# One of seven half products of the second layer as three one-pass products, in blocks 2 to 4

## The chip, the cores and the metric

The kernel runs on one core of a Trainium2 chip. The metric is the device time of one launch in microseconds (us); lower is better. Half a dozen queues work side by side on that core: TensorE (PE, with its weight loads shown as PEld), VectorE (DVE), ScalarE (ACT), GpSimd (POOL) and SyncE (SP), which issues the DMAs.

## The reference

A state-space layer (Mamba-2 SSD, chunks of 32 tokens) is followed by a two-layer perceptron with a hard-swish. The inputs of the second part are float64 and are decoded by the kernel to float32.

```python
# x (4, 8, 768, 32), a (4, 8, 768), B and C (4, 8, 768, 16)
for c in range(nc):                                   # chunks
    cum = np.cumsum(log_a[:, :, sl], axis=-1)
    L = np.exp(cum[:, :, :, None] - cum[:, :, None, :]) * causal
    M = np.einsum('bhin,bhjn->bhij', Cc, Bc) * L
    y[:, :, sl] = M @ xc + (Cc @ state) * np.exp(cum)[..., None]
    state = decay_full * state + sum_j(Bc * xc * decay_from_j)
x = y.transpose(0, 2, 1, 3).reshape(3072, 256)        # tokens x (heads * head_dim)
h = x @ w_in                                          # (3072, 2048)
g = h * np.clip(h + 3.0, 0.0, 6.0) / 6.0
out = g @ w_out                                       # (3072, 256)
```

## The kernel before

The 768 positions are cut into six blocks, k = 0 to 5, of 128 positions; a block holds the 512 tokens of the four batches. For a block, the state-space layer gives yT, the first layer gives g for f = 0 to 15 (128 of the 2048 hidden units each; the tile gT is 128 x 16 x 512), and the second layer gives the output. While the perceptron of block k runs, the state-space layer of block c = k + 1 is worked in between, and the decays of block ahead = k + 2 are prepared. The order of all of this is written out by hand: each engine's queue is what the Python loops emit, in that order, and every engine takes its queue strictly in order.

**The first layer in parts.** From block 1 on, the first layer isn't done with four-pass float32 matmuls but with three one-pass matmuls (type F32R) per product: weights and y are split into a high part of 12 bits, a low part, and a third part `less` which holds a combination of both. `squares(k, f)` does high x high and low x low into one PSUM bank, `enlarge(k, f)` multiplies the bank by 2^12 + 1 in place (on ScalarE; for f % 4 == 3 on VectorE), and `cross(k, f)` adds less x less. `factor(k, f)` then makes g: a Relu ramp on ScalarE (`ramp`, L754) and a multiplication on VectorE (`times_ramp`, L759). The loop over f emits `squares(f)`, `cross(f - 2)`, `enlarge(f)`, `factor(f - 2)`. Six banks take turns: f0 to f3, y0, y1.

**The second layer in blocks 1 to 4.** `wide_units(k)` is a Strassen-like scheme with seven half products in place of eight. The hidden units are paired (f = 2j + e, j = 0 to 7), and g is cut into quarters a11, a12, a21, a22 by e and by the half r of the tokens. `g_sums` makes s1 = a21 + a22, a21 = a11 - a21 (in place), s2 = s1 - a11 and s4 = a12 - s2 on GpSimd, two j at a time (L818; a sum of 128 x 512). `weight_sums` makes the sums of w_out once (t, L798). A half product is eight float32 matmuls of 128x256 (`product`, L914). They go to the banks oa, ob (tag o) and oc (tag f2), and the function is a generator: it yields after each of 14 units (i = 0 to 13), and the loop behind it emits other work between them:

- after unit 0 the last cross products, factors and GpSimd's sums;
- after unit 2 (3 for c = 2) `scores(c)`, which fills the banks f0 to f3 (L530), and `multiply(c)`, four VectorE multiplications that read them (L579), bank f2 first;
- after units 3 to 6 `decay_ends`: eight exponentials on ScalarE (L385) and `ends` on GpSimd (L396), for block ahead;
- `results(c)`: `sums`, `mix` (the state-space products on TensorE, L548, L625, L503), `split_y` (y_hi on ScalarE L704, y_lo and y_less on VectorE L705, L707), `take` and `renew` (the state), `from_start(ahead)` and the loads of `rows(ahead + 1)` on SP. It stands after unit 7 for c = 2 and 3, after unit 5 for c = 4 and after unit 6 for c = 5;
- after unit 9 `turn_all(ahead)` (four to five VectorE operations), after unit 12 `lead` and `lead_on`, the first products of the next block.

Between the units, ScalarE and VectorE add up the products: `third` and L967 after unit 9 (which reads both halves of ob), `u2` and L974 after unit 11, L982 after unit 13; `turned_back` transposes into `back`, and `store` issues 16 DMAs of 16 KB on SP, after units 11 and 13. In `conceal`, GpSimd masks the decays of block ahead (L158), which a DMA brought, at f = 3 and 7 (8 and 12 in block 1).

The last block has an order of its own: its second layer is done in one-pass parts as well (`last_out`, L880), 128x256 each.

Of the kernel before, what the change touches and what calls it, by code (L numbers as in the profile page):

```python
# [8 lines left out]
FP32 = mybir.dt.float32  # L9
# [3 lines left out]
F32R = mybir.dt.float32r  # L13
AF = mybir.ActivationFunctionType
ALU = mybir.AluOpType
# [6 lines left out]
def kernel(  # L22
# [24 lines left out]
    nc = tc.nc  # L47
    P = 128
# [3 lines left out]
    NC = S // P  # L52
# [750 lines left out]
    def g_quarter(k, e, r):  # L803
        return gTs[k].rearrange("p (j e) (r i) -> p e r j i", e=2, r=2)[:, e, r]

    def g_sums(k, j0, ops=range(4)):

        if k not in gsums:
            gsums[k] = {n: loads.tile([P, NJ, 2 * P], FP32, name=f"s{n}", tag="raw", bufs=NRAW)
                        for n in (1, 2, 4)}  # L810
        js = slice(j0, j0 + 2)
        a11, a12, a21, a22 = (g_quarter(k, e, r)[:, js] for r in range(2) for e in range(2))
        s1, s2, s4 = (gsums[k][n][:, js] for n in (1, 2, 4))
        sums_ = ((s1, a21, a22, ALU.add), (a21, a11, a21, ALU.subtract),
                 (s2, s1, a11, ALU.subtract), (s4, a12, s2, ALU.subtract))
        for n in ops:
            o, p_, q_, op = sums_[n]
            nc.gpsimd.tensor_tensor(out=o, in0=p_, in1=q_, op=op)  # L818

    out_parts, g_parts, ends_ = {}, {}, {}  # L820

    def split_out(i):
# [82 lines left out]
    def wide_units(k):  # L905


        halves = [[g_quarter(k, e, r) for r in range(2)] for e in range(2)]
        g2, g4, g1 = (gsums[k][n] for n in (2, 4, 1))

        def product(bank, slot, lhs, rhs, js, clear=False):

            for j in js:
                nc.tensor.matmul(  # L914
                    out=bank[:, slot], lhsT=lhs[:, j], rhs=rhs[:, j],
                    start=(clear and j == 0), stop=True, skip_group_check=True)

        near, far = range(NJ // 2), range(NJ // 2, NJ)
        res = ffn.tile([P, 2, 2, 2 * P], FP32, name="wide")
        back = ffn.tile([P, 2, TB], FP32, name="back")  # L920

        def turned_back(m, r=None):

            if r is None:
                o, i = back[:, m], res[:, m].rearrange("p r i -> p (r i)")
            else:
                o, i = back[:, m, r * 2 * P:(r + 1) * 2 * P], res[:, m, r]
            nc.vector.transpose(out=o, in_=i)

        def store(m):  # L930
            for b in range(NB):
                r0 = b * S + k * P
                for q in range(4):
                    c0 = m * P + 32 * q
                    nc.sync.dma_start(
                        out=out[r0:r0 + P, c0:c0 + 32].rearrange("(c i) m -> i c m", i=32),
                        in_=back[32 * q:32 * q + 32, m, b * P:(b + 1) * P].rearrange(
                            "i (c m) -> i c m", m=32))

        oa, ob = (ps_o.tile([P, 2, 2 * P], FP32, name=n, tag="o") for n in ("wa", "wb"))  # L940
        product(oa, 0, w4[:, 0, 0], halves[0][0], near, clear=True)
        yield
        product(oa, 0, w4[:, 0, 0], halves[0][0], far[:-1])
        yield
        product(ob, 0, wsums[4], halves[1][1], near, clear=True)
        yield
        product(ob, 0, wsums[4], halves[1][1], far)
        yield
        oc = ps.tile([P, 2, 2 * P], FP32, name="wc", tag="f2")
        product(oc, 0, w4[:, 1, 0], halves[1][0], near, clear=True)  # L950
        yield
        product(oc, 0, w4[:, 1, 0], halves[1][0], far)
        product(oa, 0, w4[:, 0, 0], halves[0][0], far[-1:])
        nc.scalar.copy(out=res[:, 0, 0], in_=oc[:, 0])
        nc.vector.tensor_tensor(out=res[:, 0, 0], in0=oa[:, 0], in1=res[:, 0, 0], op=ALU.add)
        yield
        product(ob, 1, wsums[1], g1, near)
        yield
        product(ob, 1, wsums[1], g1, far)
        turned_back(0, 0)  # L960
        yield
        product(oc, 1, wsums[3], halves[0][1], near)
        yield
        product(oc, 1, wsums[3], halves[0][1], far)
        third, u2 = (ffn.tile([P, 1, 2 * P], FP32, name=n) for n in ("third", "u2"))
        nc.scalar.copy(out=third, in_=oc[:, 1:2])
        nc.vector.tensor_tensor(  # L967
            out=res[:, :, 1], in0=ob, in1=third.to_broadcast([P, 2, 2 * P]), op=ALU.add)
        yield
        product(oa, 0, wsums[2], g2, near)  # L970
        yield
        product(oa, 0, wsums[2], g2, far)
        nc.vector.tensor_copy(out=u2, in_=oa[:, 0:1])
        nc.vector.tensor_tensor(  # L974
            out=res[:, :, 1], in0=res[:, :, 1], in1=u2.to_broadcast([P, 2, 2 * P]), op=ALU.add)
        turned_back(0, 1)
        store(0)
        yield
        product(ob, 1, w4[:, 1, 1], g4, near)
        yield  # L980
        product(ob, 1, w4[:, 1, 1], g4, far)
        nc.vector.tensor_tensor(out=res[:, 1, 0], in0=ob[:, 1], in1=u2[:, 0], op=ALU.add)  # L982
        turned_back(1)
        store(1)
        yield
# [2 lines left out]
        load_decay(c)  # L988
        load_eto(c)

    def results(c):
        if c >= TURN:
            sums(c)
        mix(c)
        if c == 1:
            keep(c)
        split_y(c)
        if TURN <= c < NC - 1:
            take(c)
        if TURN < c < NC - 1:  # L1000
            renew(c)
# [67 lines left out]
    load_x(1)  # L1069


    weave, g_done = {}, {}
    for i in range(2, NP + 2):
        for j in range(5):
            weave.setdefault(4 * i - 8 + j, []).append(i)
# [1 line left out]
    for k in range(NC):  # L1077
        gTs[k] = ffn.tile([P, NF, TB], FP32, name="gT")
        c, ahead = k + 1, k + 2
        if k == 0:  # L1080
# [14 lines left out]
            for i in range(NP):  # L1095
                for b in range(NB):
                    first_out(b, i, c)
                    for n in w_more.get((i, b), ()):
                        next(ins[n])
                    if (i, b) == (2, 0):  # L1100
                        conceal(ahead, 0)
                        conceal(ahead, 1)
                    if (i, b) == (0, 0):
                        weights(NP + 3, 1)
                        weights(NP + 2, 1)
                        weights(NP + 3, 3)
                    elif (i, b) == (1, 3):
                        turn(c, 1)
                        wake(c)
                        turn(c, 0)  # L1110
                        load_bc(ahead)
                    elif (i, b) == (2, 3):
                        decay(ahead, 0)
                        scores(c)
                        multiply(c)
                        decay(ahead, 1)
                        renew(c)
                        next(ins[2])
                        next(ins[2])
                    elif (i, b) == (3, 1):  # L1120
                        results(c)
                        decay(ahead, 2)
                    elif (i, b) == (3, 2):
                        decay(ahead, 3)
                        from_start(ahead)
                    elif (i, b) == (3, 3):
                        for q in range(NB):
                            ends(ahead, q)
# [25 lines left out]
        for f in range(2, NF):  # L1154
# [11 lines left out]
                conceal(ahead, int(f in (7, 12)))  # L1166
            if c == NC - 1 and f in (6, 8, 9):
                next(outs_[0])
            if f == NF - 1 and k not in gsums:
                g_sums(k, 0, ())  # L1170
            if k > 1 and f in (6, 10, 14):
                g_sums(k, len(g_done.setdefault(k, [])) * 2)
                g_done[k].append(f)
            if k == 1:
                if f in (4, 5, 7):
                    next(ins[3])
# [5 lines left out]
        for i, _ in enumerate(wide_units(k)):  # L1182
            if i == 0:
                cross(k, NF - 1)
                factor(k, NF - 2)
                factor(k, NF - 1)
                for n in range(4):
                    for j in range(len(g_done.get(k, [])) * 2, NJ, 2):
                        g_sums(k, j, (n,))
                if k == 1:  # L1190
                    next(more)
            if c < NC:
                if i == (3 if c == TURN else 2):
                    scores(c)
                    multiply(c)
                if ahead < NC and 3 <= i < 7:
                    decay_ends(ahead, i - 3)
                if i == {TURN: 7, TURN + 1: 7, TURN + 2: 5}.get(c, 6):
                    results(c)
                    if ahead < NC:  # L1200
                        from_start(ahead)
                    if ahead + 1 < NC:
                        rows(ahead + 1)
                if c == NC - 1:
                    for _ in range({5: 2, 8: 1, 9: 2, 10: 1, 11: 1}.get(i, 0)):
                        next(outs_[i // 8])
                if i == 9 and c == TURN:
                    renew(c)
# [36 lines left out]
```

## Time and profile before

| | |
|---|---|
| median of 3 runs | 340.27 us (340.24 to 340.45) |
| the profiled execution, its own time | 339.78 us |
| its span, first to last instruction | 337.6 us |
| TensorE busy, of the span | 330.6 us (98%) |
| VectorE, ScalarE, GpSimd busy | 234.5, 199.4, 123.9 us |
| granted TensorE clock | 1.00 |
| first layer of block 2 (137.6 to 157.6 us) | VectorE 12.3, ScalarE 14.3, GpSimd 12.4 us busy |
| second layer of block 2 (157.6 to 189.0 us) | VectorE 16.5, ScalarE 13.3, GpSimd 14.5 us busy |

The span is counted in microseconds from the first instruction; all positions in the text are on that scale. A block from 2 to 4 takes 51.1 to 51.2 us, so a place in block 2 is found 51.1 us later in block 3 and about 102.3 us later in block 4. A busy time is the union of an engine's instructions; a four-pass float32 matmul leaves two records, a one-pass matmul one.

### The profile page before, as it was taken

Reading aid. Unit: us, or ns where it says so; the run is one execution under the profiler, and the core shown is the slowest. Engines: PE = TensorE matmul, PEld = TensorE weight load, DVE = VectorE, ACT = ScalarE, POOL = GpSimd, SP = SyncE. Lnnn points to the kernel's source line nnn. Section 1 sums busy time; section 2 is a strip of 40 time slices with the busy share of each in tenths; the row PEclk is TensorE's granted clock in tenths of the full one; section 3 lists DMA queues with packets and bytes.
Section 4 is the critical chain, followed back from the end, with each engine's and each line's share of the span. In section 5 each row is a group of like instructions: output and inputs, shape, how many; then the busy total and the mean of one; then the engine's idle time right before and its main releaser. Section 6 shows DMA issues by size and latency. Waiting matters only on the chain.

```text
span 337.6 us, 8192 instructions
## 1 busy us (share of the span) xinstructions
PE 330.6 (98%) x3337; PEld 265.4 (79%) x3337; DVE 234.5 (69%) x380; ACT 199.4 (59%) x418; POOL 123.9 (37%) x123
## 2 busy tenths in 40 slices
PE   6999999999999999999999999999999999999996
PEld 2554448888888888888888888888888888899995
DVE  6699999998399739755339556355477355599974
ACT  4769878757986670576461576570486030577661
POOL 3300000290184799089813079911079800000000
PEclk9999999999999999999999999999999999999999
DMA  8999968042590215258107267101160001110001
GB/s 174 165 316 201 208 219 184 2 54 76 139 142 1 57 37 139 33 72 78 33 13 156 33 83 69 28 4 17 27 81 2 2 2 18 26 21 2 1 2 62
DMA packets 89605, 25.15 MB, mean 75 GB/s; under 512 B 82208, under 2 KB 85952, under 8 KB 89056
## 3 DMA queue, kind: packets, MB, share of 16 engines
q1 hardware_dynamic: 85184, 23.33, 37.5%
q10 hardware_dynamic: 4384, 1.31, 1.8%
q8 instruction: 26, 0.43, 0.5%
q14 instruction: 11, 0.09, 0.1%
HBM read 21.33 MB, written 3.29 MB: 73 GB/s over the span
## 4 chain that ended last, share of the span: by engine, by line
PE 94%; DMA 3%; DVE 1%; SPq 1%; issue 0%; DVEq 0%
PE h L715 33%; PE wb L914 13%; PE wc L914 8%; PE o L772 8%; PE h L647 8%; PE wa L914 8%; PE o_end L880 6%; PE y L625 3%; PE y L503 2%; PE cb L530 2%; DMA raw<-in_moe_w_in_dram 2%; DMA pairs<-in_C_dram 1%; PE y L548 1%; SPq L101 1%; PE o_end L898 1%; PE sp L548 0%
## 5 line engine op out<-in xcount | busy, mean ns | idle before, releaser
L759 DVE SCALAR_TENSOR_TENSOR gT<-gT,h 128x512 f32<-128x512 f32 x96 | 64.8, 684 | 33.8 <-ACT gT L754 32.2
L754 ACT ACTIVATE gT<-h,half 128x512 f32<-128x512 f32 x96 | 65.2, 685 | 25.6 <-PE h L715 23.6
L735 ACT ACTIVATE h<-h 128x512 f32<-128x512 f32 x66 | 38.2, 585 | 39.0 <-PE h L715 38.8
L715 PE MATMUL h<-y_hi,w_part 128*128 128x512 f32 x160 | 51.5, 407 | 0.0
L715 PE MATMUL h<-y_less,w_part 128*128 128x512 f32 x160 | 50.1, 399 | 0.0
L715 PE MATMUL h<-y_lo,w_part 128*128 128x512 f32 x160 | 49.5, 395 | 0.0
L818 POOL TENSOR_TENSOR s<-gT 128x512 f32<-128x512 f32 x16 | 23.8, 1490 | 46.7 <-DVE gT L759 46.7
L715 PEld LDWEIGHTS h<-y_lo,w_part 128*128 128x128 f32 x160 | 30.0, 188 | 7.3
L715 PEld LDWEIGHTS h<-y_hi,w_part 128*128 128x128 f32 x160 | 30.0, 188 | 6.8 <-DVE gT L759 0.2
L715 PEld LDWEIGHTS h<-y_less,w_part 128*128 128x128 f32 x160 | 29.2, 188 | 6.0 <-ACT h L735 0.2
L385 ACT ACTIVATE L<-L,cum_n 128x64 f32<-128x64 f32 x128 | 31.6, 336 | 0.0
L772 PE MATMUL o<-w_out,gT 128*128 128x256 f32 x128 | 28.8, 381 | 0.0
L647 PE MATMUL h<-yT,w_in 128*128 128x512 f32 x64 | 27.7, 594 | 0.0
L772 PEld LDWEIGHTS o<-w_out,gT 128*128 128x128 f32 x128 | 24.1, 190 | 3.8 <-issue 0.5
L647 PEld LDWEIGHTS h<-yT,w_in 128*128 128x128 f32 x64 | 12.1, 190 | 14.9 <-issue 13.2
L158 POOL TENSOR_SCALAR_AFFINE_SELECT L<-L 64x1024 f32<-64x1024 f32 (+1 forms) x16 | 20.4, 1281 | 8.5 <-DMA L<-cum_d 8.0
L579 DVE TENSOR_TENSOR L<-L,cb 128x512 f32<-128x512 f32 x24 | 15.0, 681 | 11.7 <-PE cb L530 11.7
L403 POOL TENSOR_TENSOR tmp<-state,eto 128x256 f32<-128x256 f32 x5 | 3.2, 643 | 52.8 <-ACT eto L389 48.9
L818 POOL TENSOR_TENSOR s<-gT,s 128x512 f32<-128x512 f32 x16 | 21.7, 1364 | 0.9
L396 POOL TENSOR_TENSOR bs<-B,L 128x128 f32<-128x128 f32 x24 | 11.2, 486 | 29.5 <-ACT L L385 20.9
L880 PE MATMUL o_end<-v_pair,g_pair 128*128 128x256 f32 x120 | 21.1, 281 | 0.0
L818 POOL TENSOR_TENSOR gT<-gT 128x512 f32<-128x512 f32 x16 | 20.4, 1279 | 0.9
(140 smaller groups left out, 593.0 us busy)
## 6 DMA issues: line engine op xcount, KB each, us to landing
raw<-in_moe_w_out_dram SPq DMA_DIRECT2D x4, 1024.0 KB
L<-cum_d SPq DMA_DIRECT2D x8, 512.0 KB
xt<-in_x_dram SPq DMA_DIRECT2D x6, 512.0 KB
raw<-in_moe_w_in_dram SPq DMA_DIRECT2D x3, 1024.0 KB
out_dram<-back SPq DMA_DIRECT2D x128, 16.0 KB
pairs<-in_C_dram SPq DMA_DIRECT2D x40, 32.0 KB
eto<-cum_e SPq DMA_DIRECT2D x20, 64.0 KB
B<-in_B_dram SPq DMA_DIRECT2D x5, 256.0 KB
```

Source lines behind the costliest of these rows:

```text
L158: nc.gpsimd.affine_select(out=t[rows], in_=t[rows], pattern=pattern, compare_op=ALU.is_ge, fill=-1e5, base=base, channel_multiplier=-1)
L385: nc.scalar.activation(Ls[c][:, b, h], Ls[c][:, b, h], AF.Exp, bias=cum_n[:, c, g:g + 1])
L579: nc.vector.tensor_tensor(out=Ls[c][:, :, hs], in0=Ls[c][:, :, hs], in1=cbs[c][q], op=ALU.mult)
L647: nc.tensor.matmul(out=h, lhsT=w_in[f // FP][:, j, f % FP * P:(f % FP + 1) * P], rhs=yTs[k][:, j].rearrange("p b i -> p (b i)"), start=(j ...
L715: nc.tensor.matmul(out=hs_[k, f], lhsT=w[j][:, f % FP * P:(f % FP + 1) * P], rhs=y[:, j], start=(start and j == 0), stop=True, skip_group_ ...
L735: nc.scalar.activation(h, h, AF.Copy, scale=1.0 / EPS + 1.0)
L754: nc.scalar.activation(gTs[k][:, f], h, AF.Relu, bias=half, scale=1.0 / 6.0)
L759: nc.vector.scalar_tensor_tensor(out=g, in0=g, scalar=1.0, in1=h, op0=ALU.min, op1=ALU.mult)
L772: nc.tensor.matmul(out=o[:, b % 2], lhsT=gTs[0][:, f, b * P:(b + 1) * P], rhs=w_out[:, f], start=(f == 0 and b % 2 == 0), stop=True, skip_ ...
L818: nc.gpsimd.tensor_tensor(out=o, in0=p_, in1=q_, op=op)
L880: nc.tensor.matmul(out=ends_["cross" if n == 2 else "squares"][b], lhsT=g_parts[t][n][:, b * P:(b + 1) * P], rhs=w, start=(t == 0 and b < ...
L914: nc.tensor.matmul(out=bank[:, slot], lhsT=lhs[:, j], rhs=rhs[:, j], start=(clear and j == 0), stop=True, skip_group_check=True)
```

## The change

In blocks 2 to 4 the half product t4 x a22 (unit 2 and 3 of `wide_units`) is no longer done by eight four-pass matmuls. t4 is split once into three parts (`split_sum`, in block 2), a22 in each block (`split_quarter`), and `exact` does 24 one-pass matmuls: high x high and low x low as unit 6, an enlarging of the bank's half by ScalarE, and less x less as unit 8. Product t1 x s1 takes the places of units 2 and 3. The sum s4 is written over a22, once the parts are made, so the first three of GpSimd's four sums stay where they were and the fourth moves behind unit 3. `results` is cut in two: `own_products` (sums and mix) stays, for c = 5 one unit earlier, and the rest moves behind unit 8. The parts live in tiles that are free at that time (wide, back, y_hi's, y_lo's and y_less's, cT's), so the result tiles wide and back are made only after unit 8, and the first transpose into back moves behind the rest of results.

```diff
     def g_sums(k, j0, ops=range(4)):
-        s1, s2, s4 = (gsums[k][n][:, js] for n in (1, 2, 4))
+        s1, s2, s4 = gsums[1][:, js], gsums[2][:, js], a22 if k > 1 else gsums[4][:, js]
...
+    def split_sum():
+        pair = loads.tile([P, 2, NJ, P], F32R, name="t_pair", tag="raw", bufs=NRAW)
+        hi, lo, t = pair[:, 0], pair[:, 1], wsums[4]
+        cuts = [slice(i * NJ // 2, (i + 1) * NJ // 2) for i in range(2)]
+        for sl in cuts:
+            nc.scalar.activation(hi[:, sl], t[:, sl], AF.Copy, scale=(1.0 - EPS / 2) * EPS)
+            yield
+            nc.vector.scalar_tensor_tensor(
+                out=lo[:, sl], in0=hi[:, sl].bitcast(FP32), scalar=-1.0 / EPS, in1=t[:, sl],
+                op0=ALU.mult, op1=ALU.add)
+            yield
+        less = const.tile([P, NJ, P], F32R, name="t_less", tag=f"w{NP - 1}")
+        for sl in cuts:
+            nc.gpsimd.tensor_tensor(
+                out=less[:, sl], in0=lo[:, sl].bitcast(FP32), in1=hi[:, sl].bitcast(FP32),
+                op=ALU.subtract)
...
+            yield
+
+    def split_quarter(k):
...
+        halves = [g_quarter(k, 1, 1)[:, j * NJ // 2:(j + 1) * NJ // 2] for j in range(2)]
+        hi, lo, less = quarter_parts[k] = [], [], []
+        homes = ((ffn, "wide"), (ffn, "back")), ((const, "w0"), (att, "y_lo"))
+        for where, g in zip(homes, halves):
+            h, l = (home(*w) for w in where)
...
+            for j in range(NJ // 2):
+                nc.scalar.activation(h[:, j], g[:, j], AF.Copy, scale=1.0 - EPS / 2)
+                nc.vector.tensor_tensor(
+                    out=l[:, j], in0=g[:, j], in1=h[:, j].bitcast(FP32), op=ALU.subtract)
+                yield
+        tag = {NC - 2: (ffn, "wide")}.get(k, (att, "cT"))
+        for l, h, where in zip(lo, hi, ((att, "y_less"), tag)):
+            less.append(home(*where))
+            nc.vector.scalar_tensor_tensor(
+                out=less[-1], in0=l.bitcast(FP32), scalar=-1.0 / EPS, in1=h.bitcast(FP32),
+                op0=ALU.mult, op1=ALU.add)
+            yield
...
+        def exact(bank, slot, *pairs):
+            for n in pairs:
+                for j in range(NJ):
+                    nc.tensor.matmul(
+                        out=bank[:, slot], lhsT=sum_parts[0][n][:, j],
+                        rhs=quarter_parts[k][n][j // (NJ // 2)][:, j % (NJ // 2)],
+                        start=False, stop=True, skip_group_check=True)
...
-        product(ob, 0, wsums[4], halves[1][1], near, clear=True)
-        yield
-        product(ob, 0, wsums[4], halves[1][1], far)
+        first_w, first_g = (wsums[1], g1) if parts_ else (wsums[4], halves[1][1])
+        product(ob, int(parts_), first_w, first_g, near, clear=True)
+        yield
+        product(ob, int(parts_), first_w, first_g, far)
...
+        if parts_:
+            exact(ob, 0, 0, 1)
+            nc.scalar.activation(ob[:, 0], ob[:, 0], AF.Copy, scale=1.0 / EPS + 1.0)
+            yield
+        else:
...
         product(oc, 1, wsums[3], halves[0][1], near)
         yield
+        if parts_:
+            exact(ob, 0, 2)
+            yield
+            res = ffn.tile([P, 2, 2, 2 * P], FP32, name="wide")
+            back = ffn.tile([P, 2, TB], FP32, name="back")
+            nc.vector.transpose(out=back[:, 0, :2 * P], in_=u1)
         product(oc, 1, wsums[3], halves[0][1], far)
...
     in the loop over f:
             if k > 1 and f in (6, 10, 14):
-                g_sums(k, len(g_done.setdefault(k, [])) * 2)
-                g_done[k].append(f)
+                g_sums(k, (f - 6) // 2, range(3))
+            if k == 2 and f in (2,3,4,5,6,8):
+                next(t_parts)
+            if k > 1 and f == 2:
+                quarters = split_quarter(k)
+            if k > 1 and f in ((12,13,14,15) if k == 2 else (12,13,14,15)):
+                next(quarters)
...
     between the units (i == 0 is after unit 0):
+                else:
+                    g_sums(k, NJ - 2, (0,))
+                    for _ in range(NJ // 2):
+                        next(quarters)
+            if k > 1 and i == 3:
+                for j, ops in ((4, (3,)), (0, (3,)), (2, (3,)), (6, (1, 2, 3))):
+                    g_sums(k, j, ops)
+            if k > 1 and i in (3, 6 if c == NC - 1 else 6):
+                next(quarters)
...
-                if i == {TURN: 7, TURN + 1: 7, TURN + 2: 5}.get(c, 6):
+                u = {TURN: 7, TURN + 1: 7, TURN + 2: 5}.get(c, 5)
+                if i == u:
+                    own_products(c)
+                if i == (max(u, 8) if c > TURN else u):
                     results(c)
...
                 if c == NC - 1:
-                    for _ in range({5: 2, 8: 1, 9: 2, 10: 1, 11: 1}.get(i, 0)):
+                    for _ in range({6: 1, 7: 1, 8: 1, 9: 2, 10: 1, 11: 1}.get(i, 0)):
                         next(outs_[i // 8])
```

More of the change, by code (lines that the diff above doesn't have):

```diff
@@ L806, in g_sums @@
     def g_sums(k, j0, ops=range(4)):
-        if k not in gsums:
-            gsums[k] = {n: loads.tile([P, NJ, 2 * P], FP32, name=f"s{n}", tag="raw", bufs=NRAW)
-                        for n in (1, 2, 4)}
+        if not gsums:
+            gsums.update({n: loads.tile([P, NJ, 2 * P], FP32, name=f"s{n}", tag="raw", bufs=NRAW)
+                          for n in (4, 1, 2)})
         js = slice(j0, j0 + 2)
         a11, a12, a21, a22 = (g_quarter(k, e, r)[:, js] for r in range(2) for e in range(2))
-        s1, s2, s4 = (gsums[k][n][:, js] for n in (1, 2, 4))
+        s1, s2, s4 = gsums[1][:, js], gsums[2][:, js], a22 if k > 1 else gsums[4][:, js]
         sums_ = ((s1, a21, a22, ALU.add), (a21, a11, a21, ALU.subtract),
@@ L818, in g_sums, with home @@
             nc.gpsimd.tensor_tensor(out=o, in0=p_, in1=q_, op=op)
+    def split_sum():
[14 more added lines that the diff above has]
+                op=ALU.subtract)
+            if sl is cuts[1]:
+                sum_parts.append((hi, lo, less))
+            yield
+    def split_quarter(k):
+        def home(pool, tag):
+            return pool.tile([P, NJ // 2, 2 * P], F32R, name="q_part", tag=tag, bufs=1)
+        halves = [g_quarter(k, 1, 1)[:, j * NJ // 2:(j + 1) * NJ // 2] for j in range(2)]
[3 more added lines that the diff above has]
+            h, l = (home(*w) for w in where)
+            hi.append(h)
+            lo.append(l)
+            for j in range(NJ // 2):
[10 more added lines that the diff above has]
+            yield
+    sum_parts, quarter_parts = [], {}
     out_parts, g_parts, ends_ = {}, {}, {}
@@ L908, in wide_units @@
         halves = [[g_quarter(k, e, r) for r in range(2)] for e in range(2)]
-        g2, g4, g1 = (gsums[k][n] for n in (2, 4, 1))
+        parts_ = k > 1
+        g2, g1 = gsums[2], gsums[1]
+        g4 = halves[1][1] if parts_ else gsums[4]
         def product(bank, slot, lhs, rhs, js, clear=False):
@@ L916, in product @@
                     start=(clear and j == 0), stop=True, skip_group_check=True)
+        def exact(bank, slot, *pairs):
[5 more added lines that the diff above has]
+                        start=False, stop=True, skip_group_check=True)
         near, far = range(NJ // 2), range(NJ // 2, NJ)
-        res = ffn.tile([P, 2, 2, 2 * P], FP32, name="wide")
-        back = ffn.tile([P, 2, TB], FP32, name="back")
+        if not parts_:
+            res = ffn.tile([P, 2, 2, 2 * P], FP32, name="wide")
+            back = ffn.tile([P, 2, TB], FP32, name="back")
         def turned_back(m, r=None):
@@ L953, in wide_units @@
         product(oa, 0, w4[:, 0, 0], halves[0][0], far[-1:])
-        nc.scalar.copy(out=res[:, 0, 0], in_=oc[:, 0])
-        nc.vector.tensor_tensor(out=res[:, 0, 0], in0=oa[:, 0], in1=res[:, 0, 0], op=ALU.add)
+        u1 = ffn.tile([P, 1, 2 * P], FP32, name="u2")[:, 0] if parts_ else res[:, 0, 0]
+        nc.scalar.copy(out=u1, in_=oc[:, 0])
+        nc.vector.tensor_tensor(out=u1, in0=oa[:, 0], in1=u1, op=ALU.add)
         yield
-        product(ob, 1, wsums[1], g1, near)
-        yield
-        product(ob, 1, wsums[1], g1, far)
-        turned_back(0, 0)
-        yield
+        if parts_:
[3 more added lines that the diff above has]
+        else:
+            product(ob, 1, wsums[1], g1, near)
+            yield
+            product(ob, 1, wsums[1], g1, far)
+            turned_back(0, 0)
+            yield
         product(oc, 1, wsums[3], halves[0][1], near)
         yield
+        if parts_:
+            exact(ob, 0, 2)
+            yield
+            res = ffn.tile([P, 2, 2, 2 * P], FP32, name="wide")
+            back = ffn.tile([P, 2, TB], FP32, name="back")
+            nc.vector.transpose(out=back[:, 0, :2 * P], in_=u1)
         product(oc, 1, wsums[3], halves[0][1], far)
@@ L989, in rows, with own_products @@
         load_eto(c)
-    def results(c):
+    def own_products(c):
         if c >= TURN:
@@ L994, in results @@
         mix(c)
+    def results(c):
         if c == 1:
@@ L1069 @@
     load_x(1)
-    weave, g_done = {}, {}
+    weave, t_parts = {}, split_sum()
     for i in range(2, NP + 2):
@@ L1168 @@
                 next(outs_[0])
-            if f == NF - 1 and k not in gsums:
+            if f == NF - 1 and k == 1:
                 g_sums(k, 0, ())
             if k > 1 and f in (6, 10, 14):
-                g_sums(k, len(g_done.setdefault(k, [])) * 2)
-                g_done[k].append(f)
+                g_sums(k, (f - 6) // 2, range(3))
[5 more added lines that the diff above has]
+                next(quarters)
             if k == 1:
@@ L1186 @@
                 factor(k, NF - 1)
-                for n in range(4):
-                    for j in range(len(g_done.get(k, [])) * 2, NJ, 2):
-                        g_sums(k, j, (n,))
                 if k == 1:
+                    for n in range(4):
+                        for j in range(0, NJ, 2):
+                            g_sums(k, j, (n,))
                     next(more)
+                else:
[7 more added lines that the diff above has]
+                next(quarters)
             if c < NC:
@@ L1197 @@
                     decay_ends(ahead, i - 3)
-                if i == {TURN: 7, TURN + 1: 7, TURN + 2: 5}.get(c, 6):
+                u = {TURN: 7, TURN + 1: 7, TURN + 2: 5}.get(c, 5)
+                if i == u:
+                    own_products(c)
+                if i == (max(u, 8) if c > TURN else u):
                     results(c)
```

## The prediction

> **What bounds the kernel now.** I read the page's busy table first, then the chain that ended last, then the chain in order of time, and last the timelines of VectorE and GpSimd around the places that the change touches.
>
> ```profile
> PE 330.6 (98%) x3337; PEld 265.4 (79%) x3337; DVE 234.5 (69%) x380; ACT 199.4 (59%) x418; POOL 123.9 (37%) x123
> ...
> PEclk9999999999999999999999999999999999999999
> ...
> PE 94%; DMA 3%; DVE 1%; SPq 1%; issue 0%; DVEq 0%
> ```
>
> TensorE makes up 94% of the chain, at the full granted clock. From 22.6 us on nothing else of any length stands in the chain until the last result. So every TensorE microsecond removed is a microsecond won, and every late operand is one lost. The other engines cost nothing until TensorE waits for them. Their order and deadlines must be followed, not their shares.
>
> The chain in order of time gives the prices (start, length, records):
>
> ```profile
> 161.05 1.73 PE wb L914 x8
> ...
> 166.32 3.45 PE wc L914 x16
> ...
> 170.20 3.45 PE wb L914 x16
> ...
> 296.42 1.43 PE o_end L880 x12
> 297.85 1.39 PE h L715 x6
> 299.24 1.44 PE o_end L880 x12
> ```
>
> A half product of eight four-pass matmuls leaves 16 records and takes 3.45 us. Twelve one-pass matmuls of the last block, 128x256 as well, take 1.43 us: 0.119 us each, with the change-over from L715 included.
>
> **Step 1, TensorE.** Per block 24 one-pass matmuls take 24 x 0.119 = 2.86 us in place of 3.45: 0.59 us less, 1.78 us in blocks 2 to 4 together. Nothing else enters its queue, and the number of units stays 14. The nearest rows bound the pitch: half the 0.2325 us of the 512-wide L715 gives 0.116 (1.97 us won in all); 0.122, the slowest pair of rows above, gives 1.6.
>
> By the Trainium skill, TensorE: Matmul & The Clock Gate, section Back-to-back issue gap, an isolated warm matmul comes every N/2.4 + 2.5 ns, an estimate of 109 ns here and 2.5 us won; the L880 rows of this trace, at 119 ns, disagree, and they decide.
>
> **Step 2, ScalarE and VectorE during the last four f of a block.** Each adds a ScalarE copy of 128x256 (419 ns in the SBUF row of L704, some 0.3 us queued) and a VectorE subtraction of 128x256 (0.42 us, 0.34 queued, L705). ScalarE idles 0.21 to 0.24 us in three of four f and 0.67 in the fourth, so its lag stays near 0.3 us. An enlarge has about 2.2 us until its cross product, and a bank some 2.5 us until it is reused. ScalarE costs nothing. The constant part of t (two copies, two subtractions of 512 columns) is hidden at the start of block 2 likewise, where VectorE idles 0.7 us per f.
>
> VectorE is not that simple, because GpSimd sums g at the same time. Rows of block 1 show how they meet:
>
> ```profile
> 105.36 1.21 DVE L798 TENSOR_TENSOR t<-w_out,t 128x1024 f32<-128x1024 f32 x1
> ...
> 105.51 2.19 POOL L818 TENSOR_TENSOR s<-gT 128x512 f32<-128x512 f32 x1 [2.44 <-DVE gT L759]
> ...
> 126.32 2.53 DVE L707 SCALAR_TENSOR_TENSOR y_less<-y_lo,y_hi 128x512 fp32r<-128x512 f32 x2
> ...
> 177.44 1.28 DVE L707 SCALAR_TENSOR_TENSOR y_less<-y_lo,y_hi 128x512 fp32r<-128x512 f32 x2
> ```
>
> The GpSimd sum that came 0.15 us after a VectorE operation with two SBUF inputs ended 1.13 us after that one ended: it stood still in between. The two y_less take 1.28 us alone, 2.53 beside sums. Operations that read PSUM beside SBUF (L759, L579) show none of this. So a new subtraction waits until the running sum (1.28 us) is over, and the next sum then waits for it: they alternate.
>
> **Step 3, block 2, where this bites.** GpSimd started block 2's sums at 144.73. The second low part of t now sits in VectorE's queue at 144.57 (behind L759's 143.96), so the sums start some 0.4 us later. Then: three sums (not four) to 149.1; t_less 1.28 to 150.4; conceal 2.33 to 152.75; the second t_less to 154.0. The second trio starts there, against 152.31 for the second four before. The four subtractions of f = 12 to 15 alternate with it; they begin about 155.3, 156.75, 158.2 and 160.9. The enlarge of f = 15, behind the third on VectorE, ends near 159.2 (157.11 + 0.69 = 157.8 before); cross 15 starts at 159.29. That just fits. The g of f = 15 ends near 162.4 instead of 161.2. The other four subtractions follow it with one sum before the second and one before the fourth: 4 x 0.3 + 2 x 1.15 = 3.5 us, to 165.95. Behind them in VectorE's queue stands this:
>
> ```profile
> 160.51 0.69 DVE L759 SCALAR_TENSOR_TENSOR gT<-gT,h 128x512 f32<-128x512 f32 x1 [1.36 <-ACT gT L754]
> 164.48 2.48 DVE L579 TENSOR_TENSOR L<-L,cb 128x512 f32<-128x512 f32 x4 [3.29 <-PE cb L530]
> ```
>
> The first of these multiplications frees bank f2, which wc takes at 166.32. It now ends near 165.95 + 0.69 = 166.65, so TensorE stands 0.35 us. The bounds: with every alternation kind, none; with one more sum ahead at enlarge and again at the second four, 1.35 us. I take 0.6, between the worked order and the worse one.
>
> In blocks 3 and 4 GpSimd has no t_less (in block 4 no conceal either). It waits for g of f = 11 when the second subtraction comes, g of f = 15 stays at 212.34, and the chain of 3.5 us ends at 215.85. The multiplication ends near 216.8 by the longer pitches, and wc starts at 217.44. No stall, 0.6 us to spare (block 4 likewise). If that is gone, it costs what passes it.
>
> **Step 4, the new hand-overs.** s1 is needed by unit 3 now, at 165.2 in block 2 for its last quarter; GpSimd gives it near 164. The sums g4 left for later need unit 12. The enlarge of bank ob, between the exact parts, waits in ScalarE's queue behind the decay of 2.0 us, which ends at 223.2 in block 3, while the first 16 one-pass matmuls end at 226.1; it ends at 226.6. Unit 7 covers it to 227.8. Behind it wait only more decay and y_hi. The low-less parts (128x1024, 1.2 us as L798, up to 2.4 with a sum ahead) come after the multiplications and at unit 6, before own_products or unit 8 need VectorE. Each: nothing.
>
> **Step 5, the moved split.** results goes to unit 8 (from 7, 5 and 6 in blocks 2 to 4) and takes y_hi, y_lo, y_less, take, renew, from_start and, in block 2, six row loads on SP. These are still ahead of the stores in SP's queue. The conceal that waits for them at 183.10 has until 195 on GpSimd. In block 3 the move is long: y_hi stands behind decay until 228.5, and y_lo, y_less, renew and the transpose follow (2.89 us in the rows from 225.2 to 228.09), then L967 ends near 233.75. Unit 12 overwrites bank ob at 233.95. I allow 0.1 us, with 0 to 0.4 as bounds. Blocks 2 and 4 keep 2 us. The stores' start slips by about 1.4 us; the tile back is written anew at f = 12, some 4 us behind the last store.
>
> **The sum** against the profiled execution (span 337.6, own time 339.78): -1.78 + 0.6 + 0.1 = -1.08, 338.7. The median of the runs stands 0.49 above that execution, so 339.2. A measurement of this kernel can tell 0.2%, 0.7 us, from no change.
>
> **Rivals.**
> *Clean.* The subtractions slip between the sums and no bank is late: 340.27 - 1.78 = 338.5. For it: all margins but one are positive in my working. Against: block 2's is negative by the worked order.
> *Eaten.* Blocks 3 and 4 stall like block 2, 0.4 to 0.6 us each, and the split of block 3 costs 0.4: about 340. For it: margins of 0.6 us beside sums of 1.28.
> *Slower by the alternation.* If each of the second four subtractions waits for a whole sum, the chain is 4 x (1.13 + 0.3) = 5.7 us; with the multiplication 6.4 against the 5.1 us from g of f = 15 to wc: 1.3 us lost in each block, 3.9 against 1.78, so 342.4. It decides from 0.6 us lost per block. For it: y_less doubled in block 1. Against: the first sum of the replaced quarter needs the second subtraction, so GpSimd is not always ready.
> *Weights not hidden.* If each one-pass matmul waits for its own weight load (188 ns in L880's rows), 24 x 0.188 = 4.5 us per product: 3 x 1.06 more, 343.4. L880's pitch of 119 ns speaks against it. The Trainium skill, TensorE: Matmul & The Clock Gate, section The mechanism, states that a weight load overlaps a running matmul only when the row groups differ, which full loads do not; this trace disagrees, 119 ns.
> *Not one-pass.* If the parts ran four passes, 24 x 0.431 = 10.3 us, 361 in all; L880's same declared type speaks against it.
>
> **Chances.** Forecast 0.45 (own range 338.9 to 339.6), clean 0.22, eaten 0.15, slower by alternation 0.13, weights 0.03, not one-pass 0.02. Faster by over 0.2% (under 339.6): nearly all of the first two, 0.65; within: 0.17; slower: 0.18. The range from 338.3, the clean case with the better pitch, to 340.9, the eaten case's worst, leaves out 0.18 above and 0.02 below.
>
> **What would show it.** In the chain, 16 records of 1.9 us and 8 of 0.95 in place of a 3.45 (step 1). VectorE subtractions of 0.42 us that show up to 1.7 (step 2). In block 2 an idle TensorE before wc, released by L579, and none in blocks 3 and 4 (step 3). L967 ending within 0.3 us of unit 12 in block 3 (step 5). I am wrong if the 24 matmuls do not take 2.8 to 2.9 us, if TensorE stands elsewhere, or if blocks 3 and 4 stand as long as block 2.

## The result, and the profile after

The changed kernel takes 338.48 us in the median of six runs (338.13 to 339.52), the kernel before 340.44 (340.24 to 340.82). The ratio is 0.9944 (95% interval 0.9929 to 0.9959), so 1.96 us faster, with 1.4 to 2.4 in the interval. The forecast was 339.2, with a range from 338.3 to 340.9 and 338.9 to 339.6 for its own case. The measured median lies inside the range, but outside the own case, at the time that the rival *clean* gives (338.5); the traces below show that it is not the clean case.

The page of the profiled execution (span 337.8 us, own time 339.52, the longest of its six runs) differs in the engines beside TensorE:

```profile
PE 330.6 (98%) x3361; PEld 265.5 (79%) x3361; DVE 261.6 (77%) x412; ACT 207.8 (62%) x447; POOL 133.3 (39%) x125
...
PE 96%; DVE 2%; DMA 1%; issue 0%
...
L855 DVE TENSOR_TENSOR q_part<-gT,q_part 128x256 fp32r<-128x256 f32 x24 | 21.5, 924 | 0.0
```

TensorE is still the chain. The 24 subtractions of a22's low parts (L855) show a mean of 924 ns, where the prediction's row for such an operation alone has 420.

The chain in order of time (start, length, records), block 2 first, then block 3. The names wa, wb and wc stand for the banks oa, ob and oc; L963 is `product`, L971 `exact`, the two records of L715 are the cross products of f = 15 (cross 15), and cb is `scores`:

```profile
158.76 1.73 PE wa L963 x8
160.49 0.58 PE h L715 x2
...
164.71 1.11 PE cb L530 x54
165.82 1.93 PE wb L963 x8
167.75 3.64 PE wc L963 x16
171.39 0.43 PE wa L963 x2
171.82 1.91 PE wb L971 x16
...
209.69 1.73 PE wa L963 x8
211.42 0.46 PE h L715 x2
...
215.53 0.98 PE cb L530 x55
...
218.43 3.45 PE wc L963 x16
...
224.98 2.10 PE wb L971 x16
227.09 1.73 PE wc L963 x8
228.81 0.96 PE wb L971 x8
```

Sixteen one-pass matmuls take 1.91 us (2.10 behind the small state-space products, whose end each product of before paid as well: 3.65 against 3.45), eight take 0.96: 0.119 to 0.120 us each. In this profile block 2 is longer than block 3 in three pieces: cross 15 (0.58 against 0.46), cb (1.11 against 0.98) and wc (3.64 against 3.45), 0.44 us together. The profiles of the same kernel below show which of the three counts.

From the first wa of a block to the first wa of the next (for block 4, to the first o_end of the last block), the lengths in the timelines of TensorE are these; the last column is the stretch from block 1's first wa to the last block's last product:

| us | block 2 | block 3 | block 4 | whole stretch | first wa of block 1 at |
|---|---|---|---|---|---|
| before | 51.14 | 51.11 | 36.61 | 227.92 | 105.91 |
| after | 50.93 | 50.53 | 36.02 | 226.54 | 107.11 |
| difference | -0.21 | -0.58 | -0.59 | -1.38 | +1.20 |

So blocks 3 and 4 gain the whole 0.59 us of step 1, and block 2 a third of it. That the two profiled spans differ by +0.2 and not by -1.4 has two reasons. The first wa of block 1 starts 1.2 us later, at places where the two kernels emit the same work. And the span ends 3.10 us behind VectorE's last instruction, against 2.74 before. The time doesn't show this second part: the execution's own time is 1.71 us longer than its span, against 2.15 before.

VectorE and GpSimd in block 2, in their timelines, show the alternation:

```profile
155.52 1.29 DVE L855 TENSOR_TENSOR q_part<-gT,q_part 128x256 fp32r<-128x256 f32 x1
156.74 0.67 DVE L759 SCALAR_TENSOR_TENSOR gT<-gT,h 128x512 f32<-128x512 f32 x1
157.33 0.92 DVE L855 TENSOR_TENSOR q_part<-gT,q_part 128x256 fp32r<-128x256 f32 x1
158.18 0.67 DVE L759 SCALAR_TENSOR_TENSOR gT<-gT,h 128x512 f32<-128x512 f32 x1
158.78 0.90 DVE L855 TENSOR_TENSOR q_part<-gT,q_part 128x256 fp32r<-128x256 f32 x1
159.60 0.69 DVE L732 TENSOR_SCALAR h<-h 128x512 f32<-128x512 f32 x1
...
160.80 0.41 DVE L855 TENSOR_TENSOR q_part<-gT,q_part 128x256 fp32r<-128x256 f32 x1
161.13 1.38 DVE L759 SCALAR_TENSOR_TENSOR gT<-gT,h 128x512 f32<-128x512 f32 x2
162.43 4.58 DVE L855 TENSOR_TENSOR q_part<-gT,q_part 128x256 fp32r<-128x256 f32 x4
166.94 2.47 DVE L579 TENSOR_TENSOR L<-L,cb 128x512 f32<-128x512 f32 x4
...
155.24 1.29 POOL L818 TENSOR_TENSOR s<-gT 128x512 f32<-128x512 f32 x1
156.61 1.37 POOL L818 TENSOR_TENSOR gT<-gT 128x512 f32<-128x512 f32 x1
157.93 1.47 POOL L818 TENSOR_TENSOR s<-s,gT 128x512 f32<-128x512 f32 x1
```

The subtraction at 155.52 meets a sum that began at 155.24; it ends 0.28 us behind that one and takes 1.29 us. The enlarge of f = 15 (L732) ends at 160.29, and cross 15 (at 160.49 in the chain) takes 0.12 us longer than in block 3. The last four subtractions take 4.58 us (3.57 in block 3), and the first multiplication, which frees bank f2, ends near 167.6: the place where wc starts.

### The profile page after: what moved, and what is told of

Its sections match the earlier page's. It is cut to its first block, busy times and chain, and to the rows that moved or that the text cites. A ratio compares the mean times of both kernels' runs of the same rounds, so it can differ in the third digit from the quotient of the medians.

```text
span 337.8 us, 8317 instructions
## 1 busy us (share of the span) xinstructions
PE 330.6 (98%) x3361; PEld 265.5 (79%) x3361; DVE 261.6 (77%) x412; ACT 207.8 (62%) x447; POOL 133.3 (39%) x125
## 4 chain that ended last, share of the span: by engine, by line
PE 96%; DVE 2%; DMA 1%; issue 0%
PE h L715 33%; PE wb L963 9%; PE wc L963 8%; PE o L772 8%; PE h L647 8%; PE wa L963 8%; PE o_end L927 6%; PE wb L971 3%; PE y L625 3%; PE y L503 2%; PE cb L530 2%; DMA pre<-in_a_dram 1%; PE d L357 1%; PE d L493 1%; PE d L348 1%; PE y L548 1%
## 5 line engine op out<-in xcount | busy, mean ns | idle before, releaser
L715 PE MATMUL h<-y_hi,w_part 128*128 128x512 f32 x160 | 51.5, 407 | 0.0
L715 PE MATMUL h<-y_less,w_part 128*128 128x512 f32 x160 | 49.9, 398 | 0.0
L715 PE MATMUL h<-y_lo,w_part 128*128 128x512 f32 x160 | 49.5, 395 | 0.0
L818 POOL TENSOR_TENSOR s<-gT 128x512 f32<-128x512 f32 x16 | 24.9, 1560 | 48.1 <-DVE gT L759 48.1
L715 PEld LDWEIGHTS h<-y_lo,w_part 128*128 128x128 f32 x160 | 30.0, 188 | 7.4
L715 PEld LDWEIGHTS h<-y_hi,w_part 128*128 128x128 f32 x160 | 30.0, 188 | 6.6 <-DVE gT L759 0.2
L715 PEld LDWEIGHTS h<-y_less,w_part 128*128 128x128 f32 x160 | 29.1, 188 | 6.2 <-DVE h L732 0.3
L818 POOL TENSOR_TENSOR gT<-gT 128x512 f32<-128x512 f32 x16 | 23.9, 1504 | 0.7
L855 DVE TENSOR_TENSOR q_part<-gT,q_part 128x256 fp32r<-128x256 f32 x24 | 21.5, 924 | 0.0
L818 POOL TENSOR_TENSOR s<-s,gT 128x512 f32<-128x512 f32 x16 | 20.6, 1294 | 0.0
L396 POOL TENSOR_TENSOR bs<-B,L 128x128 f32<-128x128 f32 x24 | 12.1, 527 | 19.5 <-ACT L L385 14.2
```

The source lines that it names most:

```text
L715: nc.tensor.matmul(out=hs_[k, f], lhsT=w[j][:, f % FP * P:(f % FP + 1) * P], rhs=y[:, j], start=(start and j == 0), stop=True, skip_group_ ...
L855: nc.vector.tensor_tensor(out=l[:, j], in0=g[:, j], in1=h[:, j].bitcast(FP32), op=ALU.subtract)
```

## The experiments

Four kernels ran together, then four more. In the table, as above, the lengths are from each kernel's timeline of TensorE; a dash stands for a kernel that was run for its profile and one time only.

| us | block 2 | block 3 | block 4 | whole stretch | first wa at | ratio to before (95%) |
|---|---|---|---|---|---|---|
| e0_again | 50.91 | 50.54 | 36.00 | 226.55 | 106.60 | 0.9969 (0.9947 to 0.9991) |
| e0_third | 50.97 | 50.53 | 36.02 | 226.60 | 107.15 | 0.9954 (0.9940 to 0.9968) |
| b_again | 51.16 | 51.12 | 36.61 | 227.96 | 106.99 | - |
| e1_four_pass | 51.49 | 51.76 | 36.61 | 228.96 | 106.58 | 1.0034 (1.0020 to 1.0048) |
| e2_no_sums | 50.50 | 50.57 | 36.02 | 226.22 | 107.18 | - |
| e3_less_early | 50.53 | 50.53 | 36.01 | 226.18 | 106.81 | 0.9951 (0.9927 to 0.9975) |
| e3_second | 50.53 | 50.53 | 36.01 | 226.52 | 106.19 | 0.9945 (0.9932 to 0.9957) |
| e4_always_ready | 52.00 | 51.14 | 36.62 | 228.82 | 107.40 | 1.0050 (1.0028 to 1.0072) |

### Both kernels again: how large is the gain, and what is the rest

No edit in e0_again, e0_third (the changed kernel) and b_again (the kernel before).

> The changed kernel itself, once more, beside the others of this call. The trace of the changed kernel is 1.38 us shorter from block 1's wide units to the last result (228.39 against 227.00 us), the runs are 1.96 us shorter in the median. Theory 1 (one-pass gain 1.78 us, block 2 loses 0.38 of it, the rest of the difference is the start of the program, which varies by 1 us from launch to launch): 1.4 us faster than before, and 227.0 us again from block 1's wide units to the last result. Rival (the profiled execution was a poor one, the kernel loses nothing): 1.8 to 2.0 us faster, and about 226.5 us on that stretch.

> The kernel of before, a second profile, to see how far the start of the program varies. Theory 1 (only the blocks after block 1 differ between the kernels): 227.9 us again from block 1's first wa to the last product of the last block, within 0.1 us, while the first wa starts anywhere from 106 to 107.6 us. Rival (the profile of before was a quick one throughout): over 228.3 us on that stretch.

> The changed kernel once more, beside the one with the early t_less. Theory 1: 1.4 us faster than before on the stretch from block 1 on, and 1.4 to 1.9 us by the runs.

The table's stretch ends where the last product starts, 0.46 us ahead of the point that the first expectation counts to. The changed kernel's stretch is 226.54, 226.55 and 226.60 us, that of before 227.92 and 227.96: theory 1, a gain of 1.38 us that repeats within 0.1. The rival of a poor profile falls. The start of the program differs by launch: the first wa of block 1 stands anywhere from 105.91 to 107.40 us in the ten profiles, 105.91 and 106.99 with the kernel before alone. The runs gave 1.96, then 1.6 (339.12 against 340.73) and 1.7 us (338.87 against 340.54). All three intervals hold 1.4 us (the first at its edge), and all three medians lie above it. What the runs show beyond 1.4 us is of the size of the start's scatter; that the start is on the mean quicker in the changed kernel wasn't shown.

The two repeats also show which piece of block 2 counts. Their chains in order of time, first e0_third, then e0_again:

```profile
160.55 0.56 PE h L715 x2
...
164.75 0.98 PE cb L530 x55
...
167.70 3.72 PE wc L963 x16
...
162.00 3.23 DVE q_part L855 x4
...
166.42 0.69 DVE L L579
...
167.15 3.72 PE wc L963 x16
```

Here cb is as short as in block 3, wc is longer (3.72 us), and block 2 is as long as in the first profile. In e0_again the chain itself runs through VectorE's last four subtractions and the multiplication to wc. In all three profiles wc starts 0.06 us behind the end of that multiplication, against 0.62 in block 3. So the multiplication sets the start of wc, and what TensorE loses ahead of it in the block, at cross 15 or at cb, comes out of the same wait and is no loss of its own.

### The product with four passes in the new order

```diff
+            for n in pairs[:1] if len(pairs) == 2 else ():
                 for j in range(NJ):
                     nc.tensor.matmul(
-                        out=bank[:, slot], lhsT=sum_parts[0][n][:, j],
-                        rhs=quarter_parts[k][n][j // (NJ // 2)][:, j % (NJ // 2)],
+                        out=bank[:, slot], lhsT=sum_parts[0][n][:, j].bitcast(FP32),
+                        rhs=quarter_parts[k][n][j // (NJ // 2)][:, j % (NJ // 2)].bitcast(FP32),
```

> The changed kernel with all its splits, moves and the enlarging, but with the product itself as eight four-pass float32 matmuls in unit 6, on the high parts alone (the low parts are made and not used, so the product's value is left out). Theory 1 (the gain is the pitch of the one-pass matmuls alone, 24 x 0.119 against 8 x 0.431 us, 0.59 per block): 1.8 us slower than the changed kernel, 0.4 us slower than before. Rival (part of the gain comes from the new order of the units or the moved split): less than 1.2 us slower than the changed kernel.

It is 2.4 us slower than the changed kernel (341.51 against 339.12; 2.42 on the stretch), where 1.8 was expected. Blocks 2 and 4 lose 0.56 and 0.59 us against the changed kernel, just the price of step 1, and block 4 is as long as before. So the gain is the passes, and none of it the order. Block 3 loses 1.23. The timelines of its TensorE, VectorE and ScalarE show where:

```profile
236.00 1.99 PE L963 MATMUL wb<-gT,w_out 128*128 128x256 f32 x8 [0.38 <-DVE wide L1039]
...
235.29 0.65 DVE L1039 TENSOR_TENSOR wide<-wb,third 128x512 f32<-128x512 f32 x1
...
228.75 0.37 ACT L1020 ACTIVATE wb<-wb 128x256 f32<-128x256 f32 x1 [4.46 <-PE wb L971]
229.03 2.00 ACT L385 ACTIVATE L<-L,cum_n 128x64 f32<-128x64 f32 x8
230.94 1.17 ACT L704 ACTIVATE y_hi<-y 128x256 fp32r<-128x256 f32 x4
```

With all eight four-pass matmuls in unit 6, the enlarge comes 1.6 us later; the decay, y_hi, y_lo and renew stand behind it in order, and the addition L1039 ends at 235.94, too late for unit 12, which overwrites its bank. That is the chain of step 5 with its margin used up, and it is the 0.6 us by which the expectation was too low.

### Without GpSimd's sums

```diff
-            nc.gpsimd.tensor_tensor(out=o, in0=p_, in1=q_, op=op)
+            if k == 1:
+                nc.gpsimd.tensor_tensor(out=o, in0=p_, in1=q_, op=op)
```

> The changed kernel without GpSimd's sums of g in blocks 2 to 4 (the products read what block 1 left there). Theory 1 (the subtractions wait for GpSimd alone): each of the 24 subtractions takes 0.42 us in place of a mean of 0.92, block 2 is 50.5 us long as with the early t_less, and blocks 3 and 4 stay as they are, 50.5 and 36.0 us to the last block's first product. Rival (VectorE is late by its own load): the subtractions are quick but block 2 stays near 50.9.

Groups of instructions of VectorE, with the mean in ns behind the busy time:

```profile
L856 DVE TENSOR_TENSOR q_part<-gT,q_part 128x256 fp32r<-128x256 f32 x24 | 9.3, 419 | 0.0
```

The products read here what block 1 left in the tiles of the sums. All 24 subtractions are back at 419 ns, block 2 at 50.50 us; blocks 3 and 4 stay. ScalarE's copies and VectorE's subtractions are all still there, so the loss of block 2 is the meeting of VectorE and GpSimd, not VectorE's or ScalarE's own load.

### The third part of t earlier

```diff
         for sl in cuts:
             nc.scalar.activation(hi[:, sl], t[:, sl], AF.Copy, scale=(1.0 - EPS / 2) * EPS)
             yield
+        for sl in cuts:
             nc.vector.scalar_tensor_tensor(
...
-            if k == 2 and f in (2,3,4,5,6,8):
+            for _ in range({2: 2, 3: 2, 4: 2}.get(f, 0) if k == 2 else 0):
                 next(t_parts)
```

> The changed kernel with one move: in block 2 the three steps of t's split come at f = 2, 3 and 4, so that GpSimd makes t_less while it idles ahead of the first sums and not between them. Theory 1 (block 2 loses 0.38 us because GpSimd is 2.6 us behind and its sums and VectorE's subtractions hold each other up): block 2 becomes like block 3, cross 15 back from 0.58 to 0.46 us, wc's first product from 3.64 to 3.45, the block 50.5 to 50.6 us in place of 50.93; 0.3 to 0.4 us faster than the changed kernel. Rival (the loss comes from VectorE's and ScalarE's own load in block 2, or from block 2's other order of units): no difference.

> The kernel with the early t_less once more, since its trace was 0.36 us shorter and its runs (339.23 against 339.12 us) did not show it. Theory 1: 0.36 us shorter in the trace again; with both sets of runs, 0.2 to 0.5 us faster than the changed kernel. Rival (the runs do not gain what the trace of block 2 gains): no difference in the runs again.

GpSimd's and then VectorE's timeline, and the chain of waits in order of time, all of e3_less_early:

```profile
144.41 2.54 POOL L835 TENSOR_TENSOR t_less<-t_pair 128x512 fp32r<-128x512 f32 x2 [8.76 <-DVE t_pair L829]
146.90 1.30 POOL L818 TENSOR_TENSOR s<-gT 128x512 f32<-128x512 f32 x1
...
162.69 3.57 DVE L856 TENSOR_TENSOR q_part<-gT,q_part 128x256 fp32r<-128x256 f32 x4
...
160.24 0.47 PE h L715 x2
...
167.25 3.45 PE wc L964 x16
```

t_less now lies in GpSimd's idle time ahead of the sums. Cross 15 is back at 0.47 us, wc at 3.45, the four subtractions at 3.57 as in block 3, and block 2 at 50.53 us in both profiles: 0.40 us won, as theory 1 has it. In the second profile block 1 is 0.34 us longer (51.88 us against 51.54; the code there is the same), so the stretch doesn't show it that time; the last section shows what happened there. The runs alone don't settle it: 339.23 against 339.12 us in the first set, 338.57 against 338.87 in the second, so the 0.2 to 0.5 us that was expected of both sets was not met. By the traces of block 2 this is the best version that computes the whole result.

### GpSimd with a sum always ready

```diff
-                for j, ops in ((4, (3,)), (0, (3,)), (2, (3,)), (6, (1, 2, 3))):
+                for j, ops in ((6, (1, 2)), (4, (3,)), (0, (3,)), (2, (3,)), (6, (3,))):
                     g_sums(k, j, ops)
```

> The changed kernel with another order of GpSimd's sums behind unit 3: a21 and s2 of the last two j first, which need no subtraction of VectorE, and the s4 sums after them. So GpSimd always has a sum ready while VectorE makes the last four subtractions. Theory 1 (strict alternation with whole sums): one sum more, about 1.15 us, before bank f2 comes free; block 2 stands 1.15 us longer, blocks 3 and 4, which have about 0.8 us to spare, 0.4 us each: 1.9 to 2.1 us slower than the changed kernel, and the four subtractions take 4.7 us in block 3 in place of 3.57. Rival (the engines share bandwidth, each only slowed in part, or GpSimd has priority only at the start): under 0.5 us.

Timelines of VectorE in blocks 2 and 3, and of TensorE in blocks 2 and 4:

```profile
162.72 5.65 DVE L855 TENSOR_TENSOR q_part<-gT,q_part 128x256 fp32r<-128x256 f32 x4
168.29 2.47 DVE L579 TENSOR_TENSOR L<-L,cb 128x512 f32<-128x512 f32 x4
...
214.83 4.65 DVE L855 TENSOR_TENSOR q_part<-gT,q_part 128x256 fp32r<-128x256 f32 x4
...
169.02 3.29 PE L963 MATMUL wc<-gT,w_out 128*128 128x256 f32 x14 [1.12 <-DVE L L579]
...
271.26 1.99 PE L963 MATMUL wc<-gT,w_out 128*128 128x256 f32 x8 [0.33 <-DVE L L579]
```

The four subtractions take 4.65 us in block 3 in place of 3.57 (4.7 expected) and 5.65 in block 2 in place of 4.58: one whole sum more each time. TensorE waits for L579 in all three blocks, 1.12 us in block 2 and about 0.33 in block 4. The blocks grow by 1.07 to 1.09, 0.61 and 0.60 us, 2.3 in all, against 1.9 to 2.1 expected; by the runs it is 2.95 us slower than e0_again, and slower than before. The waiting for whole sums, one by one, holds; a bandwidth shared in part falls. Whether two GpSimd sums stand ahead of three others or behind them decides whether this change is a gain.

## Why the prediction was right, and where it was off

*Step 1* held: 0.119 us per one-pass matmul in place, 0.59 us in blocks 3 and 4 each, and e1_four_pass takes just that away again in blocks 2 and 4. With it fall the rivals of weights not hidden (0.19 us each) and of four passes. The estimate of 109 ns from the Trainium skill, TensorE: Matmul & The Clock Gate, section Back-to-back issue gap, stands against 119 ns measured here, 9% more, and the measurement decides. The bound of 0.122 us comes out of none of the rows shown, which give 0.120 at most.

*Step 2* held with the mechanism: ScalarE costs nothing (e2_no_sums keeps its copies, and block 2 is clean there), and the subtractions wait out whole sums: 0.41 to 1.54 us each, a mean of 0.92 (up to 1.7 was named).

*Step 3* was right in place and mechanism: in block 2, and there alone, bank f2 comes free too late. It was mis-sized in amount. Block 2 was to lose 0.35 us by the worked order, and I took 0.6 as a mean toward the worse order; it loses 0.38. That this is so near the worked order is in part luck, since two errors cancel in it. On the scale of before (block 2 begins 1.20 us later here) the subtractions of f = 12 to 15 began at 154.3, 156.1, 157.6 and 159.6, earlier than worked, and the g of f = 15 ended at 161.3 and not near 162.4. But of the last four subtractions three waited for a whole sum and not two (1.43, 1.49, 0.41 and 1.49 us): 4.58 us together and not 3.5. They ended at 165.8, for 165.95. The enlarge of f = 15 ended at 159.1, for 159.2, and cross 15 waited 0.12 us for it where I said that it just fits; that is no further loss, as wc waits anyway. One sign I gave was not to be seen in the changed kernel: TensorE shows no idle time before wc released by L579. A record of such a product is 0.38 us long and the next starts 0.22 us behind its start, so a start that comes 0.08 us late behind the product ahead of it, as here, leaves no gap; the wait shows as a longer piece (3.64 us). In the repeats wc came 0.21 us late and left a gap of 0.05.

*Step 3, blocks 3 and 4,* held: no stall, and a margin of 0.6 us. In block 3 the multiplication ends at 217.65 and wc's first record starts at 218.27; e4_always_ready, with 1.1 us more on VectorE, uses that up and waits.

*Step 4* held: the enlarge of ob ends at 227.5 in block 3, exact's second part starts at 228.8; nothing else waits.

*Step 5* cost nothing where I allowed 0.1 us. L1039 ended 0.6 us ahead of unit 12 (234.32 against 234.96), not 0.2. On the scale of before (block 3 begins 0.99 us later here) it ended at 233.33, where I had 233.75: y_hi began at 228.32, not 228.5, and y_less, renew and the transpose followed each other closer than in the rows. e1_four_pass shows the same chain biting.

*The sum.* By the traces 1.78 - 0.38 = 1.40, measured 1.38; I had 1.08. The term mis-sized is the 0.6 for block 2, by 0.22, and the 0.1 for block 3. The other part of the distance to 338.48 is the step from one profile to the medians: I put the changed kernel as far above its own profile as the first median of before lay above its profile (0.49 us), and the starts of the programs scatter by more than that.

The other rivals: *eaten* and *slower by the alternation* didn't come, for the reason given against the latter: the s4 sums wait for the subtractions, so GpSimd isn't always ready. e4_always_ready removes that reason, and then the kernel is slower than before by 0.5% (342.07 against 340.73). *Clean* is what the trace of e3_less_early reaches, 1.74 us less than before on the stretch. That the changed kernel's median came out at clean's 338.5 is luck: by its traces it loses 0.38 us of that.

## What to carry to other kernels

When TensorE is the chain, price a change of its passes from rows of the same shape elsewhere in the trace, and then walk the in-order queues of the other engines against the first TensorE instruction that overwrites a bank they read; that walk named the one block and the one bank that lose, where the busy shares (69% and 37%) say nothing. Its amounts are less sure than its places: errors of 1.1 us cancelled in it. Before putting VectorE operations with two SBUF inputs beside GpSimd work, count whole GpSimd instructions as the wait, and look whether GpSimd has idle time a few microseconds earlier for what stands in the way.

## What the runs showed of the hardware

A short TensorE wait costs more than the idle time that is shown for it. In e4_always_ready a wait of 0.33 to 0.34 us before wc lengthens the block by 0.60 to 0.61, and in e1_four_pass one of 0.38 lengthens block 3 by 0.64 beyond step 1: about 0.26 us on top each time. The records around the wait in block 4 of e4_always_ready (at 271.26 in the timeline above) show where it is. In an undisturbed product one record starts 0.216 us behind the other and is 0.38 long, so it starts 0.16 us ahead of the other's end. Idle time counts from that end only, and leaves those 0.16 us out. The other 0.10 us is the first record behind the wait: 0.48 us long, and the next one starts 0.32 us behind it in place of 0.216. Its cause stays open; the first product behind the small state-space products begins with such a record too (0.48 us, at 216.44 in the changed kernel).

The two engines do not always take turns. In block 1, where y_less meets sums in every kernel here, nine of the ten profiles show 2.50 to 2.58 us for the two. The tenth is that of e3_second, in the timelines of VectorE, GpSimd and TensorE:

```profile
126.60 5.39 DVE L707 SCALAR_TENSOR_TENSOR y_less<-y_lo,y_hi 128x512 fp32r<-128x512 f32 x2
...
126.87 2.49 POOL L818 TENSOR_TENSOR s<-gT,s 128x512 f32<-128x512 f32 x2
...
129.32 1.51 POOL L396 TENSOR_TENSOR bs<-B,L 128x128 f32<-128x128 f32 x4
...
132.74 1.53 PE L964 MATMUL wb<-s,w_out 128*128 128x256 f32 x6 [0.15 <-DVE wide L1040]
```

There VectorE waited from 126.60 until GpSimd had done two more sums and four further operations back to back, at 130.83, and unit 12 of block 1 came late. It is one launch and only that meeting, so how often it comes, and whether it is part of the scatter of the runs, stays open. A margin counted in turns, as in step 3, may be lost in such a launch.
